# Moving a small accumulation to another slot of the matmul stream, and reading 16 consecutive tokens per partition, in an attention-plus-PReLU kernel

## The chip, the cores and the metric

The kernel runs on one core of a Trainium2 chip. The metric is the device time of one execution in microseconds. "Before" took 617.91 us (median of 3 runs, 617.37 to 618.06). The profile is one execution; its span runs from the first to the last instruction and is about 2 us shorter than the time. Engines: PE is the tensor engine, PEld its weight loads, DVE the vector engine, ACT the scalar engine, POOL and SP the two that issue DMAs here.

## The reference

```python
# x: (4, 12480, 128) f32, inducing: (32, 128); w_in: (128, 2048), w_out: (2048, 128), alpha: (2048,)
def mab(q, kv):                      # softmax attention, scale 1/sqrt(128)
    s = scale * (q @ kv.transpose(0, 2, 1)); a = exp(s - s.max(-1)); a /= a.sum(-1)
    return a @ kv
h   = mab(inducing, x)               # per batch: 32 inducing points read all 12480 tokens
att = mab(x, h)                      # each token reads the 32 points
hid = att @ w_in                     # 49920 tokens x 2048
g   = maximum(hid, 0) + alpha * minimum(hid, 0)
out = g @ w_out                      # (49920, 128) f32
```

## The kernel before

Since `att = softmax @ h`, the kernel forms `hW = h @ w_in` once per batch, and gets 512 tokens of `hid` from the 32-row weights `rep`, four copies of the exponentials, one in each quarter of the array. PReLU is split: `alpha * hid` is linear, so its part of the output is `rep` times a 32 x 128 matrix `hA`; the rest is a ReLU times `(1 - alpha) * w_out` (`W1`).

A *group* is 512 tokens; a batch has 24, and a remainder of 192 tokens. A group has four *fills*, j = 0 to 3. A fill writes four of the six PSUM banks of the *ring*; ACT and DVE evict these with a ReLU into `gt`, and `mm2` (16 matmuls) adds `gt @ W1` into the group's accumulator. There are two accumulators, for even and odd groups. When a group's last `mm2` is through, one DVE multiply (`ob`) divides by the softmax sums, and `ob` is stored. The stream on the PE is: fill n, tasks of slot n, `mm2` of fill n-1, fill n+1, and so on.

```python
def fill(st, g, j):
    ...                                     # 4 matmuls, 4 banks
    lin = j == 2 // cp and lin_groups(st.b, g)      # even g: [g, g + 1]
    if lin:
        linear(st, lin)
    bits, pos = plan[st.b * NG + g, j]      # which engine evicts which bank; where ob goes
    for r, ps in enumerate(banks):
        if r == pos:
            flush()                         # ob of the group before, if it is due
        ...                                 # ACT or DVE: gt = relu(bank)

def linear(st, groups):                     # 8 matmuls, both accumulators in turn
    for k in range(NB):
        for r, g in enumerate(groups):
            mm(accs[(st.b * NG + g) % 2][:pp, k, :],
               st.rep[g][32 * r : 32 * r + 32, k * pp : (k + 1) * pp],
               st.hA[32 * r : 32 * r + 32, :],
               start=((r == 1 or cp > 1) and k == 0), ...)   # r == 1 clears the odd one

def a_load(st, u, pieces=1):                # 2048 tokens of x, f32 to bf16; head: pieces=2
    src = x[st.b, t0 : t0 + SUP, :].rearrange("(q p j) c -> p q (j c)", q=NQ, j=NB)
    ...                                     # on the POOL queue
```
Meanwhile phase A of the next batch is threaded in as tasks: `a_scores`, `a_accum` (both one ring bank), and for this batch `b_scores` and `b_den` (one bank each). `make_plan` is a beam search, at build time, over who evicts what and where `ob` goes; it knows the tasks' slots and the linear part's cost, but it doesn't model a wait of the linear part for `ob`.

The softmax here doesn't subtract the row's maximum and nothing guards it: scores larger than these inputs give would overflow.

## Time and profile before

| | before |
|---|---|
| time, median | 617.9 us |
| PE / DVE / ACT busy | 97 / 84 / 82% |
| first fill starts | 29.58 us |
| from first to last fill | 577.10 us |
| last fill to the end | 9.02 us |

The page of before: span, busy shares by engine, and the line of the DMA queue that POOL feeds (packets, MB, share of 16 engines).

```profile
span 615.7 us, 21682 instructions
PE 596.0 (97%) x9179; PEld 436.4 (71%) x9180; DVE 520.3 (84%) x899; ACT 507.6 (82%) x998; POOL 89.0 (14%) x151
q0 software_dynamic: 21456, 39.82, 27.7%
```

The PE is the bound, but 97% busy doesn't say what can be won, since matmuls overlap: those of `mm2` start 56 ns apart and are recorded for 0.22 us each, so most of a short wait still shows as busy. What can be read is the distance between starts. Below is the timeline of before around one linear part (columns: start in us, duration in us, engine, line of the program, operation, output<-inputs, shape, count), and then the first fill of the next group.

```profile
139.74 0.38 PE L94 MATMUL ring_85<-rep,hW 32*128 32x512 bf16 x1
...
140.86 0.68 DVE L446 TENSOR_TENSOR ob<-acc_88,rd 128x512 f32<-128x512 f32 x1
141.07 0.38 PE L94 MATMUL ring_83<-rep,hW 32*128 32x512 bf16 x1
...
141.29 0.21 PE L94 MATMUL acc_87<-hA,rep 32*128 32x128 bf16 x1
141.60 0.21 PE L94 MATMUL acc_88<-hA,rep 32*128 32x128 bf16 x1
...
141.91 0.41 PE L94 MATMUL ring_81<-xn,e1T 128*32 128x128 bf16 x16
...
143.57 0.25 PE L94 MATMUL ring_86<-pick,e_2583 128*128 128x4 bf16 x4
143.69 1.05 PE L94 MATMUL acc_87<-W_169,gt 128*128 128x128 bf16 x16
144.21 0.59 ACT L395 ACTIVATE gt<-ring_83 128x512 bf16<-128x512 f32 x1
144.67 0.38 PE L94 MATMUL ring_81<-rep,hW 32*128 32x512 bf16 x1
144.68 0.39 PE L94 MATMUL ring_82<-rep,hW 32*128 32x512 bf16 x1
144.85 0.37 PE L94 MATMUL ring_83<-rep,hW 32*128 32x512 bf16 x1
```

What to see. From fill to fill (139.74 to 141.07) it is 1.33 us. The linear's first matmul, into `acc_87`, starts at 141.29; the second, into `acc_88`, only at 141.60. `ob`, which reads `acc_88`, ran from 140.86 to 141.54. The PE stood for 0.3 us. At 144.67 is a *ring wait*: two matmuls of the fill go at once, the third 0.17 us later, when ACT's eviction of its bank, `ring_83`, has ended (144.80). The profile's list of waits doesn't name either cause; it puts 104 us of PEld idle time down to "issue".

The head of before: the last wait for x, and the steps before the first fill. The bracket names what ended the idle time of that engine.

```profile
22.16 0.62 PE L156 MATMUL ring_84<-ident,xn 128*128 128x128 bf16 x8 [0.29 <-DMA xn<-in_x_dram]
28.17 0.40 PE L94 MATMUL ring_85<-w_in_b,hT_501 128*32 128x512 bf16 x4
28.62 0.69 DVE L284 CAST hW<-ring_85 128x512 bf16<-128x512 f32 x1 [0.37 <-PE ring_85 L94]
28.93 0.60 ACT L327 ACTIVATE rep<-ring_86 128x512 bf16<-128x512 f32 x1 [0.40 <-PE ring_85 L94]
29.58 0.37 PE L94 MATMUL ring_81<-rep,hW 32*128 32x512 bf16 x1 [0.24 <-ACT rep L327]
```

```profile
607.77 0.54 POOL L451 DMA_DIRECT2D out_dram<-ob  x1 [3.78 <-DVE ob L446]
...
609.55 0.32 SPq L451 DMA_DIRECT2D out_dram<-ob  x1
```

Where the text gives nanoseconds, they come from the same records before rounding to 0.01 us.

### The profile page before, as it was taken

What the parts mean: (1) busy time and instruction counts of PE and PEld (TensorE: products, weight loads), DVE (VectorE), ACT (ScalarE), POOL (GpSimd) and SP (SyncE); (2) the same over time, 40 slices, a digit from 0 to 9 for tenths busy, and PEclk for the clock granted to TensorE, in tenths of its full rate; (3) what the DMA queues carried; (4) which work ended last, traced back from release to release, by engine and by line L of the source; (5) the groups of instructions that cost most, each with busy time, mean ns of one, the idle gap of its engine ahead of it and who ended that gap; (6) DMA issues with size and microseconds to landing.
All of it is one profiled execution on the core that took longest, in us unless ns stands there. A gap on an engine that the chain in (4) does not pass through costs nothing. (4 is left out here: it accounts for less than half of the span.)

```text
span 615.7 us, 21682 instructions
## 1 busy us (share of the span) xinstructions
PE 596.0 (97%) x9179; PEld 436.4 (71%) x9180; DVE 520.3 (84%) x899; ACT 507.6 (82%) x998; POOL 89.0 (14%) x151
## 2 busy tenths in 40 slices
PE   5899999999999999999999999999999999999995
PEld 4577776777777777777777777777777777777774
DVE  4588888888888888888989898888888888888884
ACT  3688888888888888888888888888888888888884
POOL 7142112010011111110111111100101110110010
PEclk9999999999999999999999999999999999999998
DMA  9824999742125689972123599986112231221211
GB/s 142 172 69 93 185 168 169 155 115 69 65 85 129 137 151 175 155 160 88 56 80 94 112 185 164 162 154 138 53 60 76 87 96 46 87 96 45 88 56 43
DMA packets 87457, 68.66 MB, mean 111 GB/s; under 512 B 53200, under 2 KB 80736, under 8 KB 87360
## 3 DMA queue, kind: packets, MB, share of 16 engines
q0 software_dynamic: 21456, 39.82, 27.7%
q1 hardware_dynamic: 65904, 27.45, 23.5%
q8 instruction: 72, 1.18, 0.9%
q14 instruction: 25, 0.20, 0.1%
HBM read 39.94 MB, written 28.62 MB: 111 GB/s over the span
## 5 line engine op out<-in xcount | busy, mean ns | idle before, releaser
L94 PEld LDWEIGHTS <-gt 128*128 128x128 bf16 x6272 | 352.5, 98 | 73.6 <-issue 67.7
L94 PE MATMUL acc_87<-W_169,gt 128*128 128x128 bf16 (+1 forms) x3136 | 208.9, 220 | 0.0
L94 PE MATMUL acc_88<-W_169,gt 128*128 128x128 bf16 (+1 forms) x3136 | 208.8, 220 | 0.0
L451 POOL DMA_DIRECT2D out_dram<-ob x99 | 53.6, 541 | 501.8 <-DVE ob L446 445.0
L395 ACT ACTIVATE gt<-ring_84 128x512 bf16<-128x512 f32 (+1 forms) x162 | 96.9, 598 | 18.2 <-ACT gt L395 14.6
L395 ACT ACTIVATE gt<-ring_82 128x512 bf16<-128x512 f32 (+1 forms) x159 | 95.4, 600 | 14.8 <-ACT gt L395 9.7
L94 PE MATMUL ring_83<-rep,hW 32*128 32x512 bf16 (+1 forms) x269 | 101.1, 379 | 0.0
L94 PE MATMUL ring_84<-rep,hW 32*128 32x512 bf16 (+1 forms) x270 | 101.1, 378 | 0.0
L94 PE MATMUL ring_86<-rep,hW 32*128 32x512 bf16 (+1 forms) x267 | 100.4, 379 | 0.0
L94 PE MATMUL ring_81<-rep,hW 32*128 32x512 bf16 (+1 forms) x265 | 99.6, 379 | 0.7 <-ACT gt L395 0.4
L395 ACT ACTIVATE gt<-ring_86 128x512 bf16<-128x512 f32 (+1 forms) x149 | 89.2, 599 | 13.3 <-ACT gt L395 8.8
L94 PE MATMUL ring_85<-rep,hW 32*128 32x512 bf16 (+1 forms) x266 | 99.5, 378 | 0.0
L94 PE MATMUL ring_82<-rep,hW 32*128 32x512 bf16 (+1 forms) x263 | 98.8, 379 | 0.0
L395 ACT ACTIVATE gt<-ring_81 128x512 bf16<-128x512 f32 (+1 forms) x143 | 85.7, 599 | 15.5 <-ACT gt L395 11.6
L395 ACT ACTIVATE gt<-ring_85 128x512 bf16<-128x512 f32 x147 | 88.2, 600 | 11.4 <-ACT gt L395 7.8
L395 ACT ACTIVATE gt<-ring_83 128x512 bf16<-128x512 f32 (+1 forms) x142 | 84.9, 598 | 11.6 <-ACT gt L395 6.5
L397 DVE TENSOR_SCALAR gt<-ring_83 128x512 bf16<-128x512 f32 (+1 forms) x122 | 83.5, 685 | 12.0 <-PE ring_84 L94 5.6
L397 DVE TENSOR_SCALAR gt<-ring_81 128x512 bf16<-128x512 f32 (+1 forms) x117 | 80.1, 685 | 12.4 <-PE ring_83 L94 3.8
L397 DVE TENSOR_SCALAR gt<-ring_86 128x512 bf16<-128x512 f32 x113 | 77.6, 687 | 13.3 <-PE ring_81 L94 8.2
L397 DVE TENSOR_SCALAR gt<-ring_85 128x512 bf16<-128x512 f32 (+1 forms) x113 | 77.1, 683 | 11.2 <-PE ring_81 L94 4.4
L397 DVE TENSOR_SCALAR gt<-ring_84 128x512 bf16<-128x512 f32 x102 | 70.1, 688 | 12.1 <-PE ring_85 L94 6.2
L397 DVE TENSOR_SCALAR gt<-ring_82 128x512 bf16<-128x512 f32 x99 | 68.0, 687 | 11.2 <-PE ring_83 L94 5.6
(330 smaller groups left out, 388.1 us busy)
## 6 DMA issues: line engine op xcount, KB each, us to landing
out_dram<-ob POOLq DMA_DIRECT2D x96, 256.0 KB, 2.7
rep<-e2d SPq DMA_DIRECT2D x92, 128.0 KB, 3.4
xn<-in_x_dram POOLq DMA_DIRECT2D x18, 512.0 KB, 6.3
xn<-in_x_dram POOLq DMA_DIRECT2D x12, 256.0 KB, 7.2
w_out_f<-in_moe_w_out_dram POOLq DMA_DIRECT2D x1, 1024.0 KB, 14.2
w_in_b<-in_moe_w_in_dram POOLq DMA_DIRECT2D x1, 512.0 KB, 12.2
xT<-xn SPq DMA_TRANSPOSE x18, 6.6
out_dram<-ob POOLq DMA_DIRECT2D x3, 96.0 KB, 2.0
```

Source lines behind the costliest of these rows:

```text
L94: return pin(nc.tensor.matmul(o, lhsT, rhs, start=start, stop=stop, **kw))
L395: pin(nc.scalar.activation(out=gt[:, r, :w], in_=ps[:, :w], func=RELU))
L397: pin(nc.vector.tensor_relu(gt[:, r, :w], ps[:, :w]))
L451: pin((nc.sync if last_one else nc.gpsimd).dma_start(out=out[t0 : t0 + pp * nb, :].rearrange("(p j) c -> p j c", j=nb), in_=ob[:pp, :nb, :],))
```

## The change

Three ideas in one: (1) the linear part, and `a_accum` with it, go to the last fill of an even group, where the odd accumulator is long free; (2) each partition takes 16 consecutive tokens, so that a read of x is one run of 8 KB (4 KB in the head, where loads are cut in two) in place of 2 KB runs, and outputs go out as 2 KB rows 8 KB apart; (3) in the head the first scores go ahead of `hW`, whose copy is cut so that the first fill waits for a quarter of it.

```diff
-            src = x[...].rearrange("(q p j) c -> p q (j c)", q=NQ, j=NB)
+            src = x[...].rearrange("(p q j) c -> p q (j c)", q=NQ, j=NB)
...
+        for j0, j1 in ((0, 1), (1, NJ)) if first else ((0, NJ),):
+            pin(nc.vector.tensor_copy(                      # hW, in two parts at first
...
-        lin = j == 2 // cp and lin_groups(st.b, g)
+        lin = j == NJ // cp - 1 and lin_groups(st.b, g)
...
-            out=out[t0 : t0 + pp * nb, :].rearrange("(p j) c -> p j c", j=nb),
+            dst = out[t0 : t0 + SUP, :].rearrange("(p q j) c -> q p j c", q=NQ, j=nb)[q]
...
-    h_weights(st)
     b_scores_pe(st, 0, 0)
+    h_weights(st, first=True)
...
-    at(k + 8, lambda n=n, u=u: a_accum(states[n], u), 2, (240, "D", 220))
+    at(k + 8, lambda n=n, u=u: a_accum(states[n], u), 3, (240, "D", 220))
...                                                         # in make_plan:
-            lin = 240 if j == 2 // cp and lin_groups(b, g) else 0
+            lin = 240 if j == NJ // cp - 1 and lin_groups(b, g) else 0
```

More of the change, by code (lines that the diff above doesn't have):

```diff
@@ L121, in a_load @@
             xn = xn_pool.tile([P, NQ, GRP], bf16, name="xn", tag="xn")
-            src = x[st.b, t0 : t0 + SUP, :].rearrange("(q p j) c -> p q (j c)", q=NQ, j=NB)
+            src = x[st.b, t0 : t0 + SUP, :].rearrange("(p q j) c -> p q (j c)", q=NQ, j=NB)
             w = NQ // pieces
@@ L274, in h_transpose, with h_weights @@
         st.hT = st.hT4[:, 0:M]
-    def h_weights(st):
+    def h_weights(st, first=False):
         ps = bank()
@@ L283, in h_weights @@
         st.hW = work.tile([P, NJ, P], bf16, name="hW", tag="hW")
-        pin(nc.vector.tensor_copy(out=st.hW[:].rearrange("m j k -> m (j k)"), in_=ps[:]))
+        for j0, j1 in ((0, 1), (1, NJ)) if first else ((0, NJ),):
+            pin(nc.vector.tensor_copy(
+                out=st.hW[:, j0:j1, :].rearrange("m j k -> m (j k)"),
+                in_=ps[:, j0 * P : j1 * P],
+            ))
     def h_linear(st):
@@ L448, in finish @@
         ))
-        t0 = st.b * N + g * GRP
+        t0 = st.b * N + s * SUP
+        if s < NS:
+            dst = out[t0 : t0 + SUP, :].rearrange("(p q j) c -> q p j c", q=NQ, j=nb)[q]
+        else:
+            dst = out[t0 : t0 + REM, :].rearrange("(p j) c -> p j c", j=nb)
         last_one = (st.b, g) == (B - 1, NG - 1)
-        pin((nc.sync if last_one else nc.gpsimd).dma_start(
-            out=out[t0 : t0 + pp * nb, :].rearrange("(p j) c -> p j c", j=nb),
-            in_=ob[:pp, :nb, :],
-        ))
+        pin((nc.sync if last_one else nc.gpsimd).dma_start(out=dst, in_=ob[:pp, :nb, :]))
         st.rep.pop(g)
```

## The prediction

> **What bounds the kernel now.** The tensor engine: the page gives PE 97% busy, DVE 84%, ACT 82%. Busy is not peak, so I read start-to-start distances in the timeline: after most "fills" (4 matmuls of hW by rep into 4 banks) the next begins exactly 1326 ns later, 327 ns for the fill and 999 ns for the 16 matmuls of gt by W1. Evictions (ACT 0.60 us, DVE 0.69 us) mostly hide under that. What is left is where the PE stands still:
>
> 1. *The linear part.* In the third fill of an even group, 8 small matmuls add rep by hA into both accumulators. The second starts 303 ns after the first, 52 ns after the DVE's 0.68 us output multiply (ob) of the group before frees the other accumulator. From the linear's start to the next matmul block it takes 612 to 615 ns; in six cases without the wait 318 ns. 40 of about 50 wait: 40 x 297 ns = 11.9 us, all lost PE time, since nothing overtakes the waiting matmul (Trainium skill, "TensorE: Matmul & The Clock Gate", Part 3, "strict FIFO, no reordering"; this trace agrees).
> 2. *Ring waits.* With one extra bank used after an even group's last fill, the next fill's last matmuls wait 175 to 185 ns in groups with remainder 3: about 24 x 175 ns = 4.2 us.
> 3. *The head*, 29.6 us before the first fill. Loads of x bind it at both ends (4 PE waits on xn, 2.5 us).
>
> **The change, costed.**
> - Linear one fill later: ob ended 251 ns after the old start, the new start is 1.33 us later, so the wait goes; no matmul is added. Gain 12 us. Even-group fills 2 to 3 at 1326 ns should hold: odd groups already do that after the same ob.
> - Linear (217 ns net), a_accum (337 ns) and scores or denominators now share the last slot, so evictions get over 0.5 us more before the next fill: item 2 should mostly vanish (+2.5 us, up to 4). One slot per batch with three extra banks may cost 0.4 us in all.
> - 16 tokens per partition: reads merge from 2 KB to 4 KB (head) or 8 KB. POOL issue falls from 0.74 us (two-dimensional) to about 0.55 us (as w_in_b, one-dimensional), so the identity, made after four issues, is ready 0.7 us sooner. The rate hardly moves: the head already takes 205 GB/s of bf16, 410 GB/s of f32 read, against the 435 GB/s "fabric ceiling" of the Trainium skill ("DMA: Bandwidth & Descriptors", Specifications). Perhaps 1 us of head. Later loads and strided output writes are off the path.
> - Head order: scores' ACT (0.60 us) starts one matmul block earlier, and the first fill needs a 128-column copy instead of 0.69 us: 0.3 us.
>
> Sum: 12 + 2.5 + 1.3 - 0.4 = 15.4 us off 617.9.
>
> **Predicted: 602.5 us, 599.5 to 606.5 (8 in 10). Faster by over 2%: 0.82; within 2%: 0.17; slower: 0.01.**
>
> **What would show it.** Timeline: the linear's 8 matmuls start within 175 ns, and linear to next block takes 320 ns. Even-group fill 3 to 4 at 1326 ns. First fill at 28.3 us instead of 29.6. Remainder-3 ring wait below 50 ns.
>
> **What would make it wrong.** The waits come back as ring waits, because DVE and ACT lose the 0.5 to 0.85 us breather in the third fill (six fills in a row at 1326 ns, not five); then 606 to 609. Or the recomputed eviction plan puts ob elsewhere. Or the head is bound by the PE/ACT chain and gains nothing.

## The result, and the profile after

The changed kernel took 599.57 us (median of 6 runs, 597.82 to 600.42); before, run beside it, 617.84 us. The ratio is 0.970, with a 95% interval of 0.9685 to 0.972. Ratios are the mean time of one kernel's fast runs over that of the other's in the same rounds, so not quite the ratio of the medians. The gain is 18.3 us where 15.4 was predicted. The predicted range began at 599.5 us: the median is just inside it, the mean of the six runs, 599.36 us, just below.

```profile
span 597.0 us, 21696 instructions
PE 583.0 (98%) x9180; PEld 435.2 (73%) x9180; DVE 521.1 (87%) x903; ACT 507.1 (85%) x995; POOL 83.0 (14%) x151
q0 software_dynamic: 13008, 39.82, 26.5%
```

The same work, to 1 us, on DVE and ACT, in a span 18.7 us shorter. The PE's busy time fell by 13.0 us for the same matmuls: that much of the waits had counted as busy. POOL's queue moved the same 39.82 MB in 13008 packets instead of 21456. The timeline of the changed kernel around the same linear part, down to the next group's first fill:

```profile
137.49 0.68 DVE L451 TENSOR_TENSOR ob<-acc_88,rd 128x512 f32<-128x512 f32 x1
...
139.03 0.38 PE L94 MATMUL ring_81<-rep,hW 32*128 32x512 bf16 x1
...
139.25 0.21 PE L94 MATMUL acc_87<-hA,rep 32*128 32x128 bf16 x1
139.25 0.21 PE L94 MATMUL acc_88<-hA,rep 32*128 32x128 bf16 x1
...
139.57 0.25 PE L94 MATMUL ring_85<-pick,e_2567 128*128 128x4 bf16 x4
...
141.09 0.39 PE L94 MATMUL ring_81<-rep,hW 32*128 32x512 bf16 x1
...
141.10 0.38 PE L94 MATMUL ring_84<-rep,hW 32*128 32x512 bf16 x1
```

`ob` has ended 1.08 us before the linear part; its first two matmuls start together, and 0.32 us after them comes the next block. The next group's fill, at 141.09, has all its banks: four starts within 0.01 us. The head and the end of the changed kernel:

```profile
21.91 0.62 PE L156 MATMUL ring_84<-ident,xn 128*128 128x128 bf16 x8 [0.40 <-DMA xn<-in_x_dram]
28.24 0.40 PE L94 MATMUL ring_86<-w_in_b,hT_501 128*32 128x512 bf16 x4
28.34 0.60 ACT L332 ACTIVATE rep<-ring_85 128x512 bf16<-128x512 f32 x1
28.69 0.76 DVE L286 CAST hW<-ring_86 128x128 bf16<-128x128 f32 x2 [0.69 <-PE ring_86 L94]
29.12 0.38 PE L94 MATMUL ring_81<-rep,hW 32*128 32x512 bf16 x1
...
590.92 0.54 POOL L460 DMA_DIRECT2D out_dram<-ob  x1 [3.77 <-DVE ob L451]
...
592.70 0.32 SPq L460 DMA_DIRECT2D out_dram<-ob  x1
```

From the last SP issue to the end it is 6.2 us in before (615.7 - 609.55), but 4.3 us here (597.0 - 592.70): an end that the change was not meant to touch has lost 1.9 us. The ledger of the two profiles (its span ends with the start of the last instruction, 0.05 us before that one's end):

| stretch | before | after | difference | predicted |
|---|---|---|---|---|
| start to first fill | 29.58 | 29.12 | -0.46 | -1.3 |
| first to last fill: waits inside the linear part | 27.47 | 15.15 | -12.32 | -12 |
| first to last fill: all else | 549.63 | 545.55 | -4.08 | -2.1 |
| last fill to end | 9.02 | 7.15 | -1.87 | 0 |
| span | 615.70 | 596.98 | -18.72 | -15.4 |

The second row sums, over the 48 eight-matmul linear parts, the time from their start to the next block's start; the first, with nothing to wait for, is the 48 by about 0.32 us that stays.

### The profile page after: what moved, and what is told of

Read it like the earlier page. It is cut to its first block, busy times and chain, and to the rows that moved or that the text cites. A ratio compares the mean times of both kernels' runs of the same rounds, so it can differ in the third digit from the quotient of the medians.

```text
span 597.0 us, 21696 instructions
## 1 busy us (share of the span) xinstructions
PE 583.0 (98%) x9180; PEld 435.2 (73%) x9180; DVE 521.1 (87%) x903; ACT 507.1 (85%) x995; POOL 83.0 (14%) x151
## 3 DMA queue, kind: packets, MB, share of 16 engines
q0 software_dynamic: 13008, 39.82, 26.5%
## 4 chain that ended last, share of the span: by engine, by line
PE 95%; DMA 3%; ACT 1%; issue 0%; POOL 0%; DVE 0%; POOLq 0%
PE acc_88 L94 33%; PE acc_87 L94 33%; PE ring_82 L94 5%; PE ring_86 L94 5%; PE ring_84 L94 5%; PE ring_81 L94 4%; PE ring_83 L94 4%; PE ring_85 L94 4%; DMA xn<-in_x_dram 3%; ACT gt L400 0%; POOL xn L125 0%; POOL xnr L130 0%; PE ring_84 L156 0%; ACT e1T L185 0%; PE ring_85 L180 0%
## 5 line engine op out<-in xcount | busy, mean ns | idle before, releaser
L400 ACT ACTIVATE gt<-ring_81 128x512 bf16<-128x512 f32 x144 | 86.2, 599 | 14.0 <-ACT gt L400 6.7
L402 DVE TENSOR_SCALAR gt<-ring_86 128x512 bf16<-128x512 f32 x115 | 79.0, 687 | 7.6 <-PE ring_82 L94 2.5
L402 DVE TENSOR_SCALAR gt<-ring_84 128x512 bf16<-128x512 f32 x104 | 71.5, 687 | 9.4 <-PE ring_86 L94 4.4
L402 DVE TENSOR_SCALAR gt<-ring_82 128x512 bf16<-128x512 f32 x101 | 69.4, 687 | 6.8 <-PE ring_83 L94 2.2
```

The costliest lines, as they stand in the source:

```text
L400: pin(nc.scalar.activation(out=gt[:, r, :w], in_=ps[:, :w], func=RELU))
L402: pin(nc.vector.tensor_relu(gt[:, r, :w], ps[:, :w]))
```

## The experiments

Theory A: the linear's wait is for `ob`'s release of the odd accumulator (12 us), and the rest in the fills is the relief of ring waits by the longer last slot. Rivals: the rest comes from moving `a_accum` or from the recomputed plan (B), or from quieter DMA (C). The end of the program needed a theory of its own (D to G).

### e1: the linear part alone

```diff
-        lin = j == 2 // cp and lin_groups(st.b, g)
+        lin = j == NJ // cp - 1 and lin_groups(st.b, g)        # and the same in make_plan
```

> Only the linear part moves to the last fill of the even group; a_accum, layout and head as before. Theory A (the 303 ns wait for ob inside the linear plus the relief of the ring wait, both from the linear's place alone): the wait is gone (8 starts within 175 ns), fills of remainder-3 groups lose most of their 175 ns ring wait; 12 us + about 3 us, so 602 to 604 us. Rival B (the ring relief comes from moving a_accum, or from the plan recomputed for it): only the 12 us, 605 to 607 us.

602.82 us (4 runs, ratio 0.976 to before): 14.8 us of the gain, as theory A has it. The first fills of the 24 remainder-3 groups (those whose number in the batch, divided by 4, leaves 3) lost 4.3 us of ring waits together, as in the full change. But a new wait came, in the third fill, where `a_accum` had stayed (timeline of e1):

```profile
233.85 0.49 PE L94 MATMUL ring<-rep,hW 32*128 32x512 bf16 x4
234.28 0.41 PE L94 MATMUL ring<-xn,e1T 128*32 128x128 bf16 x16
```

The fill's four matmuls are spread over 0.12 us, so that the next block starts 0.42 us after the fill instead of 0.325: 21 times some 97 ns, 2.0 us.

### e2: linear part and `a_accum`

```diff
-   at(k + 8, ... a_accum(states[n], u), 2, ...)     # on top of e1
+   at(k + 8, ... a_accum(states[n], u), 3, ...)
```

> Linear and a_accum moved, layout and head order as before. Theory A: fills together 16.4 us shorter as in the changed kernel, first fill still at 29.6 us: 600.5 to 602 us, or 1.8 us less where the end of the program is the short one. Rival C (the layout smooths the DMA and so brings some of the 16.4 us): 603 us or more.

601.71 us (ratio 0.974). The fills are 16.39 us shorter in its profile, to 0.01 us the figure of the full change, with the old data layout. So rival C is out for the fills, and moving `a_accum` is worth the 2.0 us that e1 had lost. What is left to 599.6 us lies outside the fills.

### e8: `a_accum` alone

> Only a_accum moves to the last slot; the linear stays in the third fill. Theory A: the linear's wait stays (40 x 297 ns); the ring wait shrinks only where an a_accum is there (24 even groups with remainder 2 less those without one): 615 to 617 us. Rival B: 613.5 us, 4 us less.

616.44 us (ratio 0.998, interval 0.9967 to 0.9997). The linear parts keep their 613 ns. The fills together gain 1.3 us, with 1.57 us gained in the first fills of the remainder-3 groups and a little lost elsewhere. Rival B's 4 us do not come from this move by itself.

### e3 and e4: the layout alone, the head's order alone

> 16 consecutive tokens per partition alone. Theory A: the head is bound by the landing of the last piece of x, 0.24 us earlier, so the first fill comes 0.2 to 0.3 us earlier and nothing else changes: 617.3 to 617.7 us. Rival C: 615 us or less.

615.39 us (ratio 0.996, interval 0.9946 to 0.9976). My own theory failed here: the layout was worth 2.2 us where 0.2 to 0.3 us was expected. The fills are no shorter (577.89 against 577.10 us). The first fill came at 28.83 us, 0.75 us earlier, and the end took 7.04 instead of 9.02 us. That is the end's gain of the full change, so it belongs to the layout.

> Replica scores ahead of hW and the copy in two parts, alone. First fill 0.2 us earlier than 29.58 us (my prediction on record said 0.3 us), nothing else: 617.5 to 617.8 us. If the order of the head mattered more, 617 us or less.

617.44 us (ratio 0.999, interval 0.998 to 1.001), first fill at 29.37 us: 0.2 us earlier, as expected and too small for the timing to resolve.

### e5 and e6: the last outputs issued by SP

On POOL, the trace has a drain instruction that starts with the last output issue and lasts to within 0.8 us of the program's end (it stands in the records; the profile's views leave it out): 7.2 us in before, e1, e2 and e4, 5.3 us in the changed kernel and e3. SP's own waits are over earlier, 3.4 us before the end in before. The six runs of the changed kernel had also come in two levels, three at 597.8 to 598.8 us and three at 600.3 to 600.4.

```diff
-        last_one = (st.b, g) == (B - 1, NG - 1)
+        last_one = st.b == B - 1 and g >= NG - 4        # these outputs go to SP
```

> The changed kernel, with the outputs of the last four groups issued by SP instead of POOL. Theory D (the last drain on POOL, which begins with its last output issue and lasted 7.2 us in the profile of before and 5.3 us in that of the changed kernel, ends the program, and comes in two lengths 1.8 us apart): the drain ends before the last output lands, the end no longer comes in two lengths, 597 to 598 us in all rounds. Rival E (the two levels of 598.4 and 600.4 us come from elsewhere): still two levels, mean 599.4 us.

> The kernel before, with the outputs of its last four groups issued by SP. Theory D: it always had the long end, so it gains more than the changed kernel does from the same edit: 2 to 3 us, 615 to 616 us. Rival E: within 0.5 us of before, 617.5 us or more.

The changed kernel with this edit took 597.58 us (597.45 to 597.82, ratio 0.968), and before with it 614.42 us (ratio 0.995): 3.1 us less than before. The fills are the same as without it (560.70 and 577.07 us); last fill to end fell to 5.76 and 5.64 us, now the same for both layouts. The drain is still there, 4.3 us long in e5 and 6.9 us in e6, but begins with POOL's now earlier last issue and is over 15.6 and 13.4 us before the end. So the POOL drain did set the end, and before paid more for it. e5 is also faster than the changed kernel, by about 1.5 to 2 us.

### e9, e10, e15: which half of the layout shortens the drain

e9 has only the new reads, e10 only the new output addresses; e15 has the new reads in batches 0 and 1 only. All three permute rows. The reference's rows differ from their batch's mean by at most 0.015% of the largest output, so this check can't see which row went where.

```diff
-   src = x[...].rearrange("(q p j) c -> p q (j c)", ...)       # e9; e15: if st.b < 2
+   src = x[...].rearrange("(p q j) c -> p q (j c)", ...)
```

> Before, with only the reads of x in the new layout; the outputs go to the old places, so the result is wrong on purpose (rows permuted). Theory F (the last drain on POOL is shorter because fewer and larger reads went through its queue: 12288 packets of x become 3840): drain 5.3 us instead of 7.2 us, 615.4 us like the whole layout. Rival G (it is where the outputs are written): drain 7.2 us, 617 us.

> Before, with only the output addresses in the new layout (2 KB rows at a distance of 8 KB); the result is wrong on purpose (rows permuted). Theory F: drain 7.2 us, 617.6 us as before. Rival G: drain 5.3 us, 615.5 to 616 us.

> Before, with the new read layout for batches 0 and 1 only (rows of these permuted on purpose; the outputs are where they were). Theory F1 (the last POOL drain grows with all the descriptors that went through its queue in the program): drain half way, about 6.3 us, 616.5 us. Theory F2 (only the reads after the program's first ones, the later ones, count): 7.2 us, 617.5 us. If it is the early reads that count: 5.4 us, 615.5 us.

| run | packets on POOL's queue | drain | last fill to end | time, median |
|---|---|---|---|---|
| before | 21456 | 7.2 us | 9.02 us | 617.5 us |
| e10, writes only | 21456 | 7.2 us | 8.96 us | 617.74 us |
| e15, reads of two batches | 17616 | 6.7 us | 8.45 us | 616.06 us |
| e9, reads only | 13008 | 5.6 us | 7.37 us | 615.47 us |
| e3, whole layout | 13008 | 5.3 us | 7.04 us | 615.39 us |

It is the reads, not the writes (theory F), and the drain falls with the number of packets that had gone through the queue; the bytes are the same. e15 lies between: about a third of the way by its drain, two thirds by its time. Each drain is one record of one profile, but they agree: where POOL issued all outputs but the last, the eight profiles with the old reads have 7.2 to 7.6 us, the five with the new reads 5.3 to 5.6. Why the drain should depend on packets long landed, no run shows; it goes on for 3.8 us after the queue's last packet in before, and 2.2 us in the changed kernel.

### e7: the change with the plan of before

```diff
-   costs = [c for _, c in tasks.get((b * NG + g, j), []) if c]      # in make_plan
+   costs = [c for c in ptasks.get((b * NG + g, j), []) if c]        # a_accum's cost in slot 2, linear's at j == 2
```

> The changed kernel with the eviction plan of before (which engine evicts which bank, and where ob goes, computed as if linear and a_accum were still in the third fill). Theory A (placement, not the plan): within 1 us of the changed kernel, 598.5 to 600.5 us. Rival B (the recomputed plan brings the 4 us of ring waits): 602 us or more.

603.03 us (ratio 0.977): 3.5 us slower than the changed kernel, so theory A's number failed and rival B's was met. But not for B's reason. The remainder-3 groups lost the same 4.3 us of ring waits as in the change, under the old plan too. The lost time appears elsewhere, in the last fill of the even groups (timeline of e7):

```profile
92.23 0.79 PE L94 MATMUL ring<-rep,hW 32*128 32x512 bf16 x4
92.66 0.40 PE L94 MATMUL acc<-hA,rep 32*128 32x128 bf16 x8
```

The fill's four matmuls take 0.79 us instead of 0.40, and the linear part starts 0.43 us after them instead of 0.226: summed over the linear parts, 4.25 us of new ring waits. The longer slot relieves the old waits; the plan has to be recomputed so that no new ones come. Since e7's plan also had the wrong idea of the bank that each fill starts with, it is not a pure test of either.

### e12 and e14: take away the linear's wait without moving it

```diff
-   for pos in (0, 2, 4) if ended else (4,):
+   for pos in (0, 2) if ended else (4,):       # e12
+   for pos in (0,) if ended else (4,):         # e14
```

> Before, the linear left in the third fill, but ob not allowed behind all four evictions: it goes first or between the second and third. Theory A (the 303 ns are the wait for ob to release the accumulator): with ob at least one DVE eviction (0.6 us) earlier the wait inside the linear vanishes, linear to next block falls from 614 to about 320 ns; the evictions of that fill end later, so part comes back as ring waits: 606 to 613 us. Rival H (the wait belongs to the place in the third fill, whatever ob does): the second start stays at 303 ns and the time at 617 us or more.

> Before, the linear left in the third fill, but ob always ahead of the four evictions of its fill (the run before this one had not moved it: ob already stood between two evictions). Theory A (the 303 ns are the wait for ob's release of the accumulator): ob ends about 0.6 us earlier, the wait inside the linear vanishes, linear to next block falls from 614 to about 320 ns; DVE's evictions of that fill come 0.6 us later and some of it returns as ring waits, 606 to 615 us. Rival H (the wait belongs to the third fill, whatever ob does): the second start stays at 303 ns, 617 us or more.

e12 failed as an experiment: 618.22 us, and `ob` still ran from 431 ns before the linear part to 250 ns after its start, since the plan had already put it between two evictions. It tells nothing. e14 put it first, and took 609.55 us (ratio 0.987). The timeline of e14 at the same place:

```profile
138.52 0.69 DVE L446 TENSOR_TENSOR ob<-acc,rd 128x512 f32<-128x512 f32 x1 [0.23 <-PE acc L94]
...
139.74 0.49 PE L94 MATMUL ring<-rep,hW 32*128 32x512 bf16 x4
139.96 0.39 PE L94 MATMUL acc<-hA,rep 32*128 32x128 bf16 x8
140.28 0.41 PE L94 MATMUL ring<-xn,e1T 128*32 128x128 bf16 x16
```

With `ob` ended at 139.21, all eight matmuls go within 0.4 us and the next block comes 0.32 us after the first. Over the kernel the linear parts lost 12.0 us (27.47 to 15.45), with no matmul moved. Of that, 4.1 us came back between fills and `mm2` (86.37 to 90.43 us), as DVE evictions behind `ob` were late. So the wait is `ob`'s release, and moving the linear part is the better cure: some 0.8 us came back in the fills of the changed kernel, against 4.1 us here.

### e11 and e13: the changed kernel again, and one more step

> The changed kernel again, unedited, for more samples of its two levels. If the levels belong to the end of the program, runs fall at about 598.4 and 600.4 us, and a profile that falls on the high one shows a POOL drain of about 7.2 us with the fills unchanged at 560.7 us. If they belong to the fills, the drain is 5.3 us in either.

599.10 us (4 runs, 598.76 to 599.17, ratio 0.970): no second level, drain 5.5 us, fills 561.40 us. The three runs at 600.4 us stay unexplained: no profile fell on one. That e5 shows no such level fits an origin in the POOL drain but does not show it.

e13 is e5 with `h_den` and `h_transpose` one fill later, out of the slot with three extra banks, where `a_accum` to `h_den` took 572 ns.

```diff
-   at(k, ... h_den(states[n]), 3, ...)               # on top of e5
+   at(k + 1, ... h_den(states[n]), 0, ...)
-   at(k + 1, ... h_transpose(states[n]), 1, ...)
+   at(k + 1, ... h_transpose(states[n]), 2, ...)
```

> The changed kernel with the last four groups' outputs on SP (597.6 us) and, besides, h_den one fill later and h_transpose one fill later, out of the one slot per batch with three extra banks, where the PE goes 572 ns from a_accum to h_den's matmul. If that wait is real: three times 0.3 to 0.4 us, 596.4 to 596.8 us. If it only moves to the next fill: 597.4 to 597.8 us.

597.04 us (596.91 to 597.9, ratio 0.967 with 0.9657 to 0.969; e5 had 0.9679 with 0.9662 to 0.9695). The fills went from 560.70 to 560.54 us: the wait moved on to the matmuls after the next fills, each 50 to 95 ns later than before. e5 and e13 are the fastest kernels and can't be told apart.

## Why the prediction was right or wrong

- **The linear part: right.** The wait for `ob`, its size and its count were read from the trace: 12 us predicted, 12.32 measured. e14 shows the cause, e1 and e7 that the place cures it, under either plan. The order that it leaned on (Trainium skill, "TensorE: Matmul & The Clock Gate", Part 3, "strict FIFO, no reordering") held: in before, in none of the 41 parts that waited did a later matmul overtake the waiting one.
- **The ring waits: right in kind, too small in size.** This term of the sum was mis-sized: "item 2 should mostly vanish (+2.5 us, up to 4)", less 0.4 us for the slot with three extra banks, 2.1 us in all. Measured: 4.08 us. The first fills of the remainder-3 groups gave 4.29 us, all of the 4.2 us estimated and a little more, those of the remainder-1 groups 0.5 us, and some 0.8 us was lost in other fills. I had the full 4.2 us from the trace and discounted it without a reason that I could name; with over 0.5 us more in that slot against a wait of 0.175 us, nothing was left to discount.
- **The end: wrong.** The step that failed is "Later loads and strided output writes are off the path." The outputs are off the path, but the reads set, through packets on POOL's queue, the length of the drain that ends the program: 1.87 us in the profiles, shown by e3 and e9 against e10. I had not looked at what lies between the last output and the end of the span, 6.2 us in before.
- **The head: too high.** 1.3 us predicted, 0.46 in the profiled run; over the profiles of five kernels or runs with both layout and order (29.12, 29.10, 28.90, 28.47, 28.76) it is 0.5 to 1.1 us. The identity was ready 0.76 us sooner, as forecast, but the head doesn't begin there: its first piece of x landed later (the first transpose waited for x to 6.92 us; in before it started at 6.15), and at the other end it waits for the last piece, 0.24 us earlier in that run (21.53 instead of 21.77 us). "The rate hardly moves" held: a piece took 1253 instead of 1281 ns. That the "fabric ceiling" is the reason is not shown: the prediction set the rate of f32 reads against it, and what arrived in SBUF was half of that, as bf16.
- **The feared ring waits in the six fills at 1326 ns hardly came** with the recomputed plan: the even groups' third fills lost 0.8 us in all. e1 and e7 show that they do come (2.0 and 4.25 us) when `a_accum` or the plan stays behind.

Sum: the end (+1.9) and the ring term (+2.0) were short, the head (-0.8) long; the timed gain of 18.3 us takes in the three runs at 600.4 us, which the profiles' 18.7 does not.

## What to carry to other kernels

In a stream that is bound by one in-order engine, look at the distances between starts, not at busy shares: a wait in front of one small instruction is a loss of the whole engine, and it is cured by moving that instruction behind other work, if the planner of the other engines is told of the move. When a wait's size and count have been read from the trace, don't discount them without a reason. And account for the whole span, also what stands between the last useful instruction and the end: here the drain of POOL's DMA queue was worth 1.9 us, unforeseen, and 3.1 us when the last outputs went to another queue.

## What the Trainium skill lacked or had wrong

- "DMA: Bandwidth & Descriptors", Anatomy of one DMA, gives a fixed cost of about 2 us per DMA from POOL. No page that I found tells of a drain of this length on POOL after the last such DMA: 7.2 us from its issue with 21456 packets through the queue, 5.3 us with 13008. Outputs on SP instead saved 3.1 us in before (e6).
- The same page, Where 436 GB/s comes from, says that for HBM to SBUF the HBM side (about 358 GB/s) binds, though the page lists measured streams above that too. The head's reads, with one core running, took 512 KB of f32 in 1281 ns, 409 GB/s, and 418 GB/s with 4 KB runs (1253 ns). What does bind them, no run shows.
- "TensorE: Matmul & The Clock Gate", Back-to-back issue gap, has some 81 ns per pair of weight load and matmul at 128 columns as the sustained figure. Here a block of 16 such pairs takes 999 ns to the next fill's start, 62 ns each, throughout.
